# A gated recurrence and a soft mixture of experts on one core: two more couples of units that share their exponential, and another order table

## The chip, the core and the metric

The program runs on one core of a Trainium2 chip, as one launch. The metric is the device time in microseconds (us); lower is better. A core has TensorE (PE in the rows, with PEld for its weight loads), VectorE (DVE), ScalarE (ACT), GpSimd (POOL) and SyncE (SP, which here issues every DMA). All data are float32.

## The reference

Two stages follow each other. The first is a gated linear recurrence along the sequence, for 4 sequences of 5056 tokens with 256 channels:

```python
log_a = 8.0 * sigmoid(r_gate) * log(clip(sigmoid(a_param), 1e-6, 1 - 1e-6))
a_t   = exp(log_a)
norm  = sqrt(maximum(1 - a_t * a_t, 1e-6))
h[t]  = a_t[t] * h[t-1] + norm[t] * sigmoid(i_gate[t]) * x[t]
```

The second takes the 20224 rows h as x of a soft mixture of 8 experts with 4 slots each:

```python
logits   = x @ phi                      # 20224 x 32
d        = softmax(logits, axis=0)      # over all tokens
slot_in  = d.T @ x                      # 32 x 256
slot_out = relu(slot_in[e] @ w1[e]) @ w2[e]
out      = softmax(logits, axis=1) @ slot_out
```

The softmax over all tokens means that no row of the output can be made before the last token has been scanned.

## The kernel before

The 20224 tokens are cut into 40 windows of 512 (the last has 256). Channels are two halves h of 128 partitions. Per window w the program lists operations, each on a given engine, and the texts below name them by these short names:

- `Lr`, `Li`, `Lx` (line 382): three loads of 512 KB on SP.
- `rp` (line 397, PE, per half): the r gate is transposed into a bank of PSUM. `sr` (line 409, ACT, per half): its sigmoid, or a tanh of half the argument, into the buffer A.
- `si` (line 420, ACT): sigmoid of the i gate. `u` (line 432, POOL): that times x.
- `ex` (lines 460 and 462, ACT): the exponential of A in place. Line 460 is used where `sr` ran as a sigmoid, with a scale per channel; line 462 where it ran as a tanh, with a scale and a bias per channel.
- `sq` (line 471, POOL): A squared into buffer N. `qr` (line 478, ACT): the square root of one minus that.
- `up` (line 490, PE, per half): u is transposed into a bank. `st` (line 500, DVE, per half): N times that. `sc` (line 513, DVE, per half): the scan, which carries its last column into the next window.
- `yp` (line 533, PE) and `yc` (lines 286 and 288, a copy on ACT or DVE, two per window): h is transposed back and copied out of PSUM.

Windows are joined to units for `si`, `ex` and `qr`: window 0, (1, 2), (3, 4), 5, and then pairs from (6, 7) to (38, 39); a unit is called by its first window. Four windows make a group g of the second stage: `lp` (line 579, PE, logits), `ls` (lines 588 to 592, DVE, their running maximum), `ep` (lines 603 and 606, PE), `ee` (line 612, ACT, exponential), `md` (line 597, ACT), `acc` (line 621, PE) and `as` (lines 630 and 632, DVE, the sum over tokens).

After the last scan come the end of the sum over tokens (lines 668 to 699: `mp`, `mx`, `mc`, `wj`, `we`, `W`, `sp`, `slot`), the experts (`hp` line 761, `ht` line 773, `so` line 788, all on PE), and then for each group the weights of its tokens (`ct` line 841, `c0` line 847, `cm`, `c1`, `c2`, `c3`), their transposition (`hc` line 865, `hx`), the product (`op` line 894) copied out by ACT or DVE (`og`), and the store (`out`).

ACT holds one table set at a time; tanh and exp are in one set, sigmoid and sqrt each in another, and the build puts a table load ahead of an instruction whose set is not the one held. `EXM` lists couples of units whose `ex` is one operation: it waits for the `sr` of both units. If both units used the same form and their buffers lie fewer than 16 pairs apart, that operation is one instruction per half for both units; otherwise each unit has its own two instructions, one unit behind the other (function `e_ex`).

The order of all operations is written out by hand: `ORDER` is a list of the operations' numbers (a "b" takes the second engine that an operation allows). `Plan.order` goes through it once, gives each operation its buffer, bank or pair from a small model of times, and then the operations are emitted in that order, so that each engine's queue is the table's order of that engine. `LAT["DMA"]` is the model's time between the end of a load's issue and its use; it enters the choice of buffers.

Of the kernel before, what the change touches and what calls it, by code (L numbers as in the profile page):

```python
# [10 lines left out]
ALU = mybir.AluOpType  # L11
# [14 lines left out]

ORDER = """
# [27 lines left out]
790 812 963 986 965 750 771 969 985 751 772 643 661 659 662 675 715 696 682 679 904 905 626 680 683 906 716 756
898 755 737 757 701 908 698 681 684 699 702 700 703 723 720 899 900 739 901 902 624b 798 685 686b 663 664b 909
704 644 705b 665 687 646 896 645b 666b 688b 647b 758 778 759 721 724 722 725 740 799 819 800 742 743 741 903 910
760 911 706 912 707 744 915 913 763 916 726 745 777 779 782 761 764 762 796 747 917 919 765 780 783 781 784 746b  # L60
727b 748b 766 768 728 1089 767b 920 918 729b 978 977 966 791 971 813 979 962 987 983 968 959 957 797 801 804 921
818 820 922 923 924 823 805 802 907 769b 914 803 806 974 972 961 824 821 825 822 982 981 958 988 960 967 976 973
964 980 984 970 785 1067 926 927 786b 807 928 787 937 938 808b 929 788 930 939 946 931 826 827b 940 947 809 810b
941 932 933 942 948 949 943 934 944 935 1090 950 1068 925 951 945 936 952 1013 1111 1035 953 1177 954 1091 990
1112 1113 1000 1114 991b 1036 1014 1037 1038 1039 995 992 996 1005 1001 997 1002 993 1069 1015 1070 1115 1016
1006 1092 998 1071 1017 994 1003 999 1007 1008 1004 1009 1178 1093 1179 1010 955 1116 1040 1018 1094 1072 1041
956 1011 1073 1042 1074 1180 1012b 1055 1056 1057 1059b 1058b 1043 1049 1044 1047 1050 1053 1046b 1045b 1061
1095 1052b 1065b 1096b 1062b 1063b 1051 1181 1064 1075 1076b 1077b 1079 1078 1082 1199 1019 1083b 1086b 1084b
1085 1200 1020 1201 1182 1104 1155 1105b 1107 1156 1097 1157 1133 1108b 1202 1106b 1098b 1099b 1028 1029b 1032b
1031b 1117 1101 1100 1134 1135 1030 1118b 1021 1022b 1024b 1136 1158 1119 1221 1183 1120b 1184b 1122b 1123b 1025  # L70
1023 1121 1159 1160 1126 1161 1127b 1162b 1129b 1128b 1222 1223 1130 1137 1185 1186 1203 1170 1189b 1187b 1188b
1138 1192 1171 1174b 1173b 1224 1172b 1193 1204 1196 1139 1163 1140b 1194b 1195b 1148 1164 1167 1165 1225 1149
1150 1205 1226 1151b 1152b 1166 1206b 1214 1215 1218 1217 1216b 1060 1048 1054 1066 1227 1228b 1141 1207 1208b
1209b 1210b 1142 1143 1145 1211 1144 1229 1236 1230 1231 1237 1240 1233 1239 1238b 1232b 1080 1081 1087 1088
1110 1103 1109 1033 1102 1034 1026 1124 1027 1125 1131 1132 1175 1191 1190 1176 1153 1197 1168 1220 1219 1147
1213 1198 1242 1234 1235 1146 1154 1212 1169 1241
"""


# [96 lines left out]
def kernel(  # L176
# [11 lines left out]
    nc = tc.nc  # L188
# [44 lines left out]
    def Bk(key):  # L233
        return banks[plan.place[key]]
# [4 lines left out]
    def halves(key):  # L239
        return G(key).rearrange("p (h t) -> p h t", h=H)  # L240
# [116 lines left out]
    def window(w):  # L357
# [148 lines left out]

        def e_sc(h):
            def emit(o):
                up = Bk(("up", w, h))
                for s0, s1 in zip(cuts[:-1], cuts[1:]):  # L510
                    init = 0.0 if (w * C + s0) % S == 0 else last_col[h]
                    dst = halves(("A", w))[:, h, s0:s1]
                    nc.vector.tensor_tensor_scan(  # L513
                        dst, dst, up[:, s0:s1], init, op0=ALU.mult, op1=ALU.add
                    )
                    last_col[h] = halves(("A", w))[:, h, s1 - 1 : s1]
            return emit

        for h in range(H):
            op(("up", w, h), "PE", 0.5 * f, e_up(h), deps=[("u", w), ("ident",)],  # L520
               alloc=[("B", ("up", w, h))], uses=[("x", w)])
            op(("st", w, h), "DVE", 0.06 + 0.54 * f, e_st(h), deps=[("up", w, h), ("qr", u0)],
               uses=[("N", w), ("up", w, h)])
            op(("sc", w, h), "DVE", 0.09 * (len(cuts) - 1) + 1.09 * f, e_sc(h),
               deps=[("st", w, h), ("sc", w - 1, h)],
               uses=[("A", w), ("up", w, h)] + ([("A", w - 1)] if w else []))

        def e_yp(i):
            def emit(o):
# [436 lines left out]
```

## Time and profile before

| | us |
|---|---|
| median of 3 runs | 302.04 |
| lowest and highest | 301.23, 302.51 |
| profiled execution, its own time | 301.67 |
| span of its instructions | 299.80 |

Busy time in that span: DVE 239.7 us (80%), ACT 242.2 (81%), PE 234.7 (78%), POOL 181.9 (61%). The DMA queue moved 100.03 MB, at 334 GB/s over the span.

The program has three stretches: up to about 218 us the windows are scanned; up to about 243.5 us the sum over tokens ends and the experts run; after that the output is made and stored. A busy share over the whole span mixes these; it says little on which engine sets the time of one of them.

### The profile page before, as it was taken

The page shows a single profiled execution, that of the slowest core. Times are in us where ns is not written, and L with a number is a line of the kernel's source. Part 1 is how long each engine was busy: PE and PEld are TensorE (multiplying, and loading weights), DVE is VectorE, ACT ScalarE, POOL GpSimd, SP SyncE. Part 2 cuts the span into 40 slices and gives each one's busy share as a digit, 9 for nine tenths or more (in the row PEclk, how much of TensorE's full clock was granted, in tenths as well). Part 3 has the DMA queues.
Part 4 walks back from the last instruction along what each step waited for, and adds up shares of the span by engine and source line. Part 5 has one row for each costly group of instructions (what it writes and reads, how often), then busy time and mean ns, then how long its engine had stood idle before and what let it go on. Part 6 is the DMA issues. An engine that isn't in the chain of part 4 may idle for free.

```text
span 299.8 us, 5788 instructions
## 1 busy us (share of the span) xinstructions
PE 234.7 (78%) x2140; PEld 166.0 (55%) x2140; DVE 239.7 (80%) x379; ACT 242.2 (81%) x303; POOL 181.9 (61%) x122
## 2 busy tenths in 40 slices
PE   3605788869896989799958996899999999898200
PEld 3505575666773967457647663557573677665100
DVE  1003999899999999989999999999968779889600
ACT  5899999999999999999999999999323248885100
POOL 4299579988498898899749898798000421121000
PEclk9975999979999899979999999999999999999755
DMA  6999999799895988859998789999991019999997
GB/s 247 416 410 407 410 397 382 306 390 359 327 416 206 416 340 330 302 200 382 331 360 318 273 302 404 385 378 380 339 398 60 3 79 402 404 402 407 404 378 297
DMA packets 28032, 100.03 MB, mean 334 GB/s; under 512 B 3362, under 2 KB 3364, under 8 KB 28004
## 3 DMA queue, kind: packets, MB, share of 16 engines
q1 hardware_dynamic: 28004, 99.66, 86.7%
q8 instruction: 17, 0.28, 0.4%
q14 instruction: 11, 0.09, 0.1%
HBM read 78.94 MB, written 20.71 MB: 332 GB/s over the span
## 4 chain that ended last, share of the span: by engine, by line
ACT 28%; PE 27%; POOL 15%; issue 12%; DVE 7%; DMA 4%; DVEq 0%; POOLq 0%; ACTq 0%
POOL g L471 8%; POOL g L432 5%; ACT g L462 4%; ACT g L420 4%; ACT g L478 4%; PE b L397 4%; ACT y L286 4%; ACT g L409 4%; PE b L894 4%; DMA g<-in_x_dram 4%; PE b L533 3%; PE b L490 3%; DVE g L288 3%; PE b L788 2%; PE b L761 2%
## 5 line engine op out<-in xcount | busy, mean ns | idle before, releaser
L432 POOL TENSOR_TENSOR g<-g 128x1024 f32<-128x1024 f32 (+1 forms) x40 | 92.7, 2344 | 18.9 <-ACT g L420 17.2
L513 DVE TENSOR_TENSOR_SCAN g<-g,b 128x512 f32<-128x512 f32 (+4 forms) x86 | 98.7, 1175 | 0.4
L471 POOL TENSOR_TENSOR g<-g 128x1024 f32<-128x1024 f32 (+1 forms) x40 | 73.8, 1873 | 17.9 <-ACT g L462 13.6
L500 DVE SCALAR_TENSOR_TENSOR b<-g,b 128x512 f32<-128x512 f32 (+1 forms) x80 | 51.8, 675 | 25.1 <-PE b L490 24.1
L490 PE MATMUL b<-ident,g 128*128 128x128 f32 x316 | 48.5, 289 | 22.0 <-POOL g L432 20.2
L490 PEld LDWEIGHTS b<-ident,g 128*128 128x128 f32 x316 | 36.3, 146 | 35.0 <-POOL g L432 23.6
L397 PE MATMUL b<-ident,g 128*128 128x128 f32 x316 | 46.7, 293 | 6.0 <-DMA g<-in_r_gate_dram 3.7
L533 PE MATMUL b<-ident,g 128*128 128x128 f32 x316 | 44.7, 284 | 8.3 <-DVE g L513 6.8
L397 PEld LDWEIGHTS b<-ident,g 128*128 128x128 f32 x316 | 37.9, 151 | 15.7 <-issue 4.2
L533 PEld LDWEIGHTS b<-ident,g 128*128 128x128 f32 x316 | 35.8, 144 | 18.8 <-DVE g L513 11.2
L409 ACT ACTIVATE g<-b 128x512 f32<-128x512 f32 (+1 forms) x80 | 42.4, 604 | 2.9 <-PE b L397 2.9
L861 POOL TENSOR_TENSOR y<-y,rs 128x512 f32<-128x512 f32 x10 | 10.4, 1047 | 53.5 <-DVE g L779 25.2
L462 ACT ACTIVATE g<-g,ca 128x1024 f32<-128x1024 f32 (+2 forms) x30 | 39.1, 1371 | 0.0
L420 ACT ACTIVATE g<-g 128x2048 f32<-128x2048 f32 (+2 forms) x22 | 37.9, 1744 | 0.1
L478 ACT ACTIVATE g<-g 128x2048 f32<-128x2048 f32 (+2 forms) x22 | 36.8, 1732 | 0.1
L288 DVE COPY y<-b 128x512 f32<-128x512 f32 x53 | 34.6, 680 | 2.1 <-PE b L533 1.5
L286 ACT COPY g<-b 128x512 f32<-128x512 f32 (+1 forms) x45 | 22.2, 567 | 8.7 <-PE b L894 8.0
L894 PE MATMUL b<-soR,y 32*128 32x256 f32 x320 | 27.2, 405 | 1.2 <-ACT y L286 0.7
L288 DVE COPY g<-b 128x512 f32<-128x512 f32 (+1 forms) x43 | 24.7, 629 | 2.5 <-ACT y L286 0.8
L286 ACT COPY y<-b 128x512 f32<-128x512 f32 x36 | 20.0, 601 | 5.7 <-PE b L533 4.4
L621 PE MATMUL b<-y,e 128*32 128x257 f32 x316 | 22.9, 388 | 1.2 <-ACT e L612 1.2
L579 PE MATMUL b<-g,phi_sb 128*32 128x512 f32 (+1 forms) x160 | 22.4, 622 | 0.0
(86 smaller groups left out, 220.2 us busy)
## 6 DMA issues: line engine op xcount, KB each, us to landing
g<-in_i_gate_dram SPq DMA_DIRECT2D x39, 512.0 KB, 7.1
g<-in_x_dram SPq DMA_DIRECT2D x39, 512.0 KB, 6.5
out_dram<-g SPq DMA_DIRECT2D x39, 512.0 KB, 6.4
g<-in_r_gate_dram SPq DMA_DIRECT2D x38, 512.0 KB, 6.5
g<-in_moe_w_dram SPq DMA_DIRECT2D x32, 512.0 KB, 6.2
g<-in_r_gate_dram SPq DMA_DIRECT2D x3, 256.0 KB, 5.0
g<-in_i_gate_dram SPq DMA_DIRECT2D x1, 256.0 KB, 4.2
g<-in_x_dram SPq DMA_DIRECT2D x1, 256.0 KB, 7.7
```

The costliest lines, as they stand in the source:

```text
L286: nc.scalar.copy(out=dst, in_=srct)
L288: nc.vector.tensor_copy(out=dst, in_=srct)
L397: nc.tensor.transpose(out=by_tile(rp, n)[:, j, :], in_=rows(("r", w), n)[:, j, h * P : (h + 1) * P], identity=ident,)
L409: nc.scalar.activation(halves(("A", w))[:, h, :c], Bk(("rp", w, h))[:, :c], f, scale=k)
L420: nc.scalar.activation(a, a, AF.Tanh if twice else AF.Sigmoid, scale=0.5 if twice else 1.0)
L432: nc.gpsimd.tensor_tensor(out=rows(("x", w), n), in0=rows(("i", w), n), in1=rows(("x", w), n), op=ALU.mult)
L462: nc.scalar.activation(a, a, AF.Exp, scale=ca[:, h : h + 1], bias=ca[:, h : h + 1])
L471: nc.gpsimd.tensor_tensor(out=halves(("N", w))[:, :, :c], in0=a, in1=a, op=ALU.mult)
L490: nc.tensor.transpose(out=by_tile(up, n)[:, j, :], in_=rows(("x", w), n)[:, j, h * P : (h + 1) * P], identity=ident,)
L500: nc.vector.scalar_tensor_tensor(up, halves(("N", w))[:, h, :c], 5e-4 if twice else 1e-3, up, op0=ALU.max, op1=ALU.mult)
L513: nc.vector.tensor_tensor_scan(dst, dst, up[:, s0:s1], init, op0=ALU.mult, op1=ALU.add)
L533: nc.tensor.transpose(out=yp[:, j, h * P : (h + 1) * P], in_=halves(("A", w))[:, h, (2 * i + j) * P : (2 * i + j + 1) * P], identity=ident,)
```

## The change

`EXM` gets two more couples, (8, 6) and (28, 24); `LAT["DMA"]` goes from 2.0 to 3.0; and `ORDER` is replaced by another table, with 1241 operations in place of 1243 since each new couple makes one `ex` of two. A second form of the step after the square root (`pooled`) is added to `window`, for windows in the list `BY_POOL`; the list is empty, so that none of its operations is made. Lines of the kernel move down by up to 27.

```diff
-EXM = [(12, 14), (18, 20), (30, 34), (36, 38)]
+EXM = [(8, 6), (12, 14), (18, 20), (28, 24), (30, 34), (36, 38)]
 LAST = 3
+BY_POOL = []
...
-LAT = {"DVE": 0.13, "ACT": 0.15, "POOL": 0.12, "PE": 0.26, "DMA": 2.0}
+LAT = {"DVE": 0.13, "ACT": 0.15, "POOL": 0.12, "PE": 0.26, "DMA": 3.0}
...
-5 1 33 55 11 115 74 96 116 34 13 56 12 75 97 138 35 137 57 178 200 76 159 98 219 241 160 179 201 117 0 3 6 7 8 9
+1 5 74 96 33 115 55 11 35 34 56 57 179 12 76 13 178 0 3 6 7 8 9 10 77 79 101 99 78 102 80 100 36 38 118 58 60 37
...
+        pooled = w in BY_POOL
+        least = 5e-4 if twice else 1e-3
...
+            if pooled:
+                continue
```

Three places show how the instructions move.

The first is ACT's queue around the exponentials of units 6, 8 and 10. Before (the table load, `ex` of 8, a sigmoid, `ex` of 6, `ex` of 10, which is the tanh form, and sigmoids):

```order
L420 ACTIVATE g<-g 128x2048
L409 ACTIVATE g<-b_76 128x512
L460 ACT_TABLE_LOAD
L460 ACTIVATE g<-g,ca_91 128x2x512 x2
L409 ACTIVATE g<-b_77 128x512
L460 ACTIVATE g<-g,ca_91 128x2x512 x2
L462 ACTIVATE g<-g,ca 128x2x512 x2
L409 ACTIVATE g<-b_76 128x512
```

With the change (lines 461, 463, 410 and 421 are the 460, 462, 409 and 420 of before; line 639 is `ee`):

```order
L421 ACTIVATE g<-g 128x2048
L461 ACT_TABLE_LOAD
L461 ACTIVATE g<-g,ca_91 128x2x2x512 x2
L410 ACTIVATE g<-b_75 128x512
L410 ACTIVATE g<-b_77 128x512
L410 ACTIVATE g<-b_76 128x512
L639 ACTIVATE e_68<-b_73 128x512
L463 ACTIVATE g<-g,ca 128x2x512 x2
```

Units 8 and 6 are now two instructions of twice the width, and `ee` of group 0 has come ahead of the exponential of unit 10.

The second is ACT's queue around the couple (12, 14). Before, one joint pair of instructions (the third row), then a sigmoid, `md`, `ee`, the second sigmoid of window 20 and `ex` of 16:

```order
L409 ACTIVATE g<-b_75 128x512
L462 ACT_TABLE_LOAD
L462 ACTIVATE g<-g,ca 128x2x2x512 x2
L409 ACTIVATE g<-b_73 128x512
L597 ACTIVATE d_127<-m_104,n_116 128x1
L612 ACTIVATE e_68<-b_77 128x512
L409 ACTIVATE g<-b_72 128x512
L462 ACTIVATE g<-g,ca 128x2x512 x2
```

With the change:

```order
L421 ACTIVATE g<-g 128x2048
L461 ACT_TABLE_LOAD
L461 ACTIVATE g<-g,ca_91 128x2x512 x2
L463 ACTIVATE g<-g,ca 128x2x512 x2
L410 ACTIVATE g<-b_73 128x512
L639 ACTIVATE e_68<-b_75 128x512
L410 ACTIVATE g<-b_71 128x512
L410 ACTIVATE g<-b_72 128x512
L624 ACTIVATE d_127<-m_104,n_116 128x1
```

The couple's two units have different forms now and are four instructions; the sigmoid right behind them is the first of window 26 (into bank b_73), which stood behind `ex` of 16 before.

The third is the end of the scans. On DVE before, around `as` of group 7 (line 632), which stands between the `st` of window 38 and its `sc`:

```order
L513 SCALAR_TENSOR_TENSOR g<-g,b_71 128x512
L500 SCALAR_TENSOR_TENSOR b_70<-g,b_70 128x512
L500 SCALAR_TENSOR_TENSOR b_74<-g,b_74 128x512
L632 SCALAR_TENSOR_TENSOR accS<-accS,d_133,b_77 128x257
L513 SCALAR_TENSOR_TENSOR g<-g,b_74 128x512
```

With the change it stands ahead of the first `st` of window 36 (the fourth row):

```order
L504 SCALAR_TENSOR_TENSOR b_75<-g,b_75 128x512
L659 SCALAR_TENSOR_TENSOR accS<-accS,d_133,b_74 128x257
L528 SCALAR_TENSOR_TENSOR g<-g,b_75 128x512
L504 SCALAR_TENSOR_TENSOR b_70<-g,b_70 128x512
L528 SCALAR_TENSOR_TENSOR g<-g,b_70 128x512
```

On PE, between the last `acc` and the experts, before (841 is `ct`, 696 is `sp`, 761 is `hp`):

```order
L841 MATMUL b_75<-ident,l_78 128x4x32 x4
L841 MATMUL b_77<-ident,l_82 128x4x32 x4
L841 MATMUL b_73<-ident,l_79 128x4x32 x4
L696 MATMUL b_74<-Wt,accS 128x32 x2
L841 MATMUL b_71<-ident,l_85 128x4x32 x4
L761 MATMUL b_74<-g,slotT 32x512 x8
```

With the change (868, 723 and 788 are the same three):

```order
L868 MATMUL b_70<-ident,l_80 128x4x32 x4
L868 MATMUL b_74<-ident,l_85 128x4x32 x4
L723 MATMUL b_71<-Wt,accS 128x32 x2
L868 MATMUL b_72<-ident,l_78 128x4x32 x4
L868 MATMUL b_71<-ident,l_81 128x4x32 x4
L788 MATMUL b_76<-g,slotT 32x512 x8
```

One `ct` has moved from ahead of `sp` to behind it.

## Rows read from the trace of the kernel before

**Rows 1.** Busy time by stretch: us, PE, PEld, DVE, ACT, POOL, PEclk, DMA share, GB/s.

```profile
27.60:201.60 174.00, 150.24 (x1281) 108.58 (x1280) 169.11 (x231) 172.89 (x185) 146.88 (x72) 0.97 0.91 345
201.60:218.40 16.80, 16.29 (x144) 10.98 (x143) 16.55 (x30) 10.88 (x19) 7.10 (x4) 1.00 0.96 354
243.50:299.80 56.30, 33.83 (x368) 23.56 (x368) 35.47 (x68) 27.18 (x56) 5.23 (x5) 0.83 0.94 369
```

**Rows 2.** Waits of ACT between 4 and 217 us: total us, times, longest us.

```profile
ACT y L286 <- PE b L533: 4.4, 2, 2.4
ACT g L409 <- PE b L397: 2.9, 4, 1.2
```

**Rows 3.** Timeline of ACT, pieces of six stretches: start us, us, what, count.

```profile
46.17 2.19 ACT L460 ACTIVATE g<-g,ca 128x1024 f32<-128x1024 f32 x2
48.27 0.57 ACT L409 ACTIVATE g<-b 128x512 f32<-128x512 f32 x1
...
132.85 2.37 ACT L462 ACTIVATE g<-g,ca 128x1024 f32<-128x1024 f32 x2
135.11 1.07 ACT L409 ACTIVATE g<-b 128x512 f32<-128x512 f32 x2
...
164.80 4.08 ACT L462 ACTIVATE g<-g,ca 128x2048 f32<-128x2048 f32 x2
168.77 2.60 ACT L409 ACTIVATE g<-b 128x512 f32<-128x512 f32 x6
...
196.05 0.35 ACT L597 ACTIVATE d<-m,n 128x1 f32<-128x1 f32 x1
196.25 2.09 ACT L286 COPY y<-b 128x512 f32<-128x512 f32 x4
198.35 1.28 ACT L478 ACT_TABLE_LOAD   x1
199.65 3.38 ACT L478 ACTIVATE g<-g 128x2048 f32<-128x2048 f32 x3
```

**Rows 4.** Timeline of DVE at the end of the scans.

```profile
201.59 1.29 DVE L500 SCALAR_TENSOR_TENSOR b<-g,b 128x512 f32<-128x512 f32 x2
...
210.79 0.48 DVE L632 SCALAR_TENSOR_TENSOR accS<-accS,d,b 128x257 f32<-128x257 f32 x1
...
218.25 0.14 DVE L661 COPY m<-m 32x1 f32<-32x1 f32 x1
```

**Rows 5.** Waits of DVE between 28 and 218 us.

```profile
DVE b L500 <- ACT g L478: 0.7, 1, 0.7
```

**Rows 6.** Timeline of ACT, its first sigmoids; in brackets the idle time before.

```profile
5.97 0.60 ACT L409 ACTIVATE g<-b 128x512 f32<-128x512 f32 x1 [1.16 <-PE b L397]
6.83 0.60 ACT L409 ACTIVATE g<-b 128x512 f32<-128x512 f32 x1 [0.26 <-PE b L397]
8.37 2.07 ACT L409 ACTIVATE g<-b 128x512 f32<-128x512 f32 x4 [0.94 <-PE b L397]
```

**Rows 7.** The chain of work that ended last, at the experts' start: start us, us, what.

```profile
222.09 1.86 PE b L841 x12
223.95 0.37 PE b L696 x4
224.32 0.54 PE b L841 x4
224.86 5.29 PE b L761 x48
```

**Rows 8.** Timeline of ACT around the couple (12, 14).

```profile
71.85 1.95 ACT L420 ACTIVATE g<-g 128x2048 f32<-128x2048 f32 x1
73.66 1.12 ACT L409 ACTIVATE g<-b 128x512 f32<-128x512 f32 x2
...
76.09 4.08 ACT L462 ACTIVATE g<-g,ca 128x2048 f32<-128x2048 f32 x2
```

**Rows 9.** The loads of line 382, from issue to landing.

```profile
DMA to landing us min/median/max: 3.3/6.6/11.7
```

More of the change, by code (lines that the diff above doesn't have):

```diff
@@ new lines @@
+598 653 613 633 618 615 616 617 619 891 890 602 604 639 892 655 636 562 603 620 581 583 634 654 635 716 736 582b
+605b 717 564 565b 584b 675 695 563 893 895 658 958 978 980 749 708 667 689 730 960 707 977 729 673 676 640 637
+641 638 642 752 644 656 659 657 660 680 681 682 902 903 694 696 699 677 748 769 789 970 770 969 966 971 965 957
+788 810 713 754 896 753 643b 894 796 904 714 735 755 906 645 678 700 697 679 698 718 897 898 701 721 899 900 901
+740 661 683 621 685 662b 684b 686b 622b 623 624b 907 702 737 663 704 905 703b 719 722 720 738 723 739 664b 908
@@ new lines @@
+909 758 910 911 761 741 913 1033 912 742 756 776 757 762 797 817 775 798 794 743 914 763 759 915 724 726 780
+744b 727b 725b 781 760 782 917 918 777 745 764 766 778 779 746b 765b 705b 767b 963 979 976 811 982 959 964 981
+967 973 987 956 961 962 955 795 802 799 919 816 803 920 821 921 922 818 1109 783 800 801 804 819 822 820 823 968
+986 975 972 984 983 985 924 925 785 935 805 936 926 806 807 928 784b 786b 927 808b 929 937 916 944 1034 939 945
+824 940 825b 946 923 930 931 932 933 947 941 942 1065 1175 1110 948 949 938 934 943 950 951 952 1011 1087 988
@@ new lines @@
+1066 1067 1111 1012 1013 989 1014 1015 1112 1003 993 990 994 998 995 1004b 1035 991 1036 999b 996 1037 1088 1089
+1090 1068 992 1000 1005 1001 997 1002 1006 1007 1113 1069 1176 1177 1091 953 954 1070 1038 1016 1092 1039 1008b
+1178 1009 1010b 1071 1072b 1040 1041 1042 1043 1047 1044b 1045b 1048 1049 1051b 1050b 1053 1059 1054b 1061b
+1063b 1093 1094b 1056 1055 1057 1060 1062 1179 1073 1074 1077 1075b 1076b 1080 1153 1017 1131 1081b 1084b 1018b
+1082b 1083b 1154 1155 1132 1133 1102 1156 1026 1103b 1105b 1106b 1104 1157 1027 1030 1029b 1028b 1095 1096b
@@ new lines @@
+1098b 1134 1099b 1097b 1180 1181 1182 1135 1197 1019 1020b 1022b 1021 1158 1136 1114 1159 1160b 1183 1137 1219
+1198 1199 1184b 1185b 1023b 1187 1190 1138 1200 1186 1220 1115 1191b 1192b 1116b 1193b 1221 1194 1146 1168 1147b
+1150b 1148b 1201 1149 1161 1169b 1172b 1171 1170 1162b 1165 1164b 1202 1163b 1203 1117 1118 1121 1204b 1120b
+1119b 1124 1125 1126 1127b 1128b 1046 1052 1058 1064 1139 1205 1222 1140b 1142b 1143b 1141 1212 1206b 1223 1208
+1213b 1215b 1207b 1224 1209 1214 1225 1216 1226 1227 1234 1235 1237 1228b 1231b 1236b 1229b 1238 1230 1078 1079
@@ L77 @@
+1085 1086 1107 1108 1031 1032 1100 1101 1024 1189 1188 1195 1196 1152 1174 1166 1173 1025 1123 1167 1129 1130
+1145 1211 1218 1122 1239 1232 1233 1144 1217 1240 1210 1151
 """
@@ L500, in emit, with e_uc, e_nm, e_pb @@
                 nc.vector.scalar_tensor_tensor(
-                    up, halves(("N", w))[:, h, :c], 5e-4 if twice else 1e-3, up, op0=ALU.max, op1=ALU.mult
+                    up, halves(("N", w))[:, h, :c], least, up, op0=ALU.max, op1=ALU.mult
                 )
             return emit
+        def e_uc(h):
+            return lambda o: copy(o, halves(("x", w))[:, h, :c], Bk(("up", w, h))[:, :c])
+        def e_nm(o):
+            nt = halves(("N", w))[:, :, :c]
+            nc.gpsimd.tensor_scalar(nt, nt, least, None, op0=ALU.max)
+        def e_pb(o):
+            b = halves(("x", w))[:, :, :c]
+            nc.gpsimd.tensor_tensor(out=b, in0=halves(("N", w))[:, :, :c], in1=b, op=ALU.mult)
         cuts = [0] + [b * S - w * C for b in range(1, B) if w * C < b * S < w * C + c] + [c]
@@ L508, in emit @@
             def emit(o):
-                up = Bk(("up", w, h))
+                b = halves(("x", w))[:, h, :] if pooled else Bk(("up", w, h))
                 for s0, s1 in zip(cuts[:-1], cuts[1:]):
@@ L513, in emit @@
                     nc.vector.tensor_tensor_scan(
[L514 removed]
+                        dst, dst, b[:, s0:s1], init, op0=ALU.mult, op1=ALU.add
                     )
@@ L526, in window @@
                uses=[("A", w), ("up", w, h)] + ([("A", w - 1)] if w else []))
+        if pooled:
+            op(("nm", w), "POOL", 0.08 + 0.95 * f, e_nm, deps=[("qr", u0)], uses=[("N", w)])
+            for h in range(H):
+                op(("uc", w, h), ("ACT", "DVE"), {"DVE": 0.06 + 0.54 * f, "ACT": 0.055 + 0.43 * f}, e_uc(h),
+                   deps=[("up", w, 0), ("up", w, 1)], uses=[("x", w), ("up", w, h)])
+            op(("pb", w), "POOL", 0.08 + 1.77 * f, e_pb, deps=[("nm", w), ("uc", w, 0), ("uc", w, 1)],
+               uses=[("N", w), ("x", w)])
+            for h in range(H):
+                op(("sc", w, h), "DVE", 0.09 * (len(cuts) - 1) + 1.09 * f, e_sc(h),
+                   deps=[("pb", w), ("sc", w - 1, h)], uses=[("A", w), ("x", w)] + ([("A", w - 1)] if w else []))
         def e_yp(i):
```

39 lines of the change are left out of this document (7 added, 32 removed), and 31 rows, old and new, of the table ORDER.

## The prediction

> **What bounds the kernel now.** I first read the busy time by stretch, then each engine's waits, then the timelines of the two engines that turned out full. The busy shares of the whole span (ACT 81%, DVE 80%) hide that between 27.6 and 201.6 us ACT is busy for 172.89 of 174.00 us and DVE for 169.11 [rows 1]. POOL and PE have room there, and the DMA share is 0.91. The waits of ACT say the same: 2.9 us in four waits for a transposed gate, and 4.4 us for y copies, which come at 213 us and later, when its main work is over [rows 2]. Of the 2.9 us, 1.16, 0.26 and 0.94 stand before its first sigmoids [rows 6], so that one wait of about 0.5 us is left for the other 190 us. DVE waited only 0.7 us for a square root [rows 5].
>
> The two engines meet at the root of unit 36. The last three roots start at 199.65 us [rows 3], the first of them takes about 1.9 us, and DVE's first `st` of window 36 starts at 201.59 us [rows 4], when DVE has just run out of earlier work. From there DVE has its last eight `st`, eight scans and the end of the maximum, to 218.25 us [rows 4], with 16.55 of 16.80 us busy [rows 1]. Then the experts follow on PE from 224.86 us [rows 7], and then the output, whose 56.3 us are DMA time (share 0.94, 369 GB/s) while ACT is busy for 27 and DVE for 35 us [rows 1]. So the time is: ACT's queue up to the root of 36, DVE's tail, the experts, the stores.
>
> **ACT's work up to that root.** Counting the order's rows to that point, both versions have 80 `sr`, 20 `si`, 20 `qr`, 8 `ee` and 22 table loads (24 in the whole program). The new couples spare no table load. What differs: one y copy more (20 for 19), four of which take 2.10 us up to the next instruction, so 0.5 [rows 3]; one `md` more, 0.20 (196.05 to 196.25) [rows 3]; and the exponentials. A joint couple in the tanh form takes 3.97 us (164.80 to 168.77), a single unit in that form 2.26 (132.85 to 135.11), a single unit in the sigmoid form 2.10 (46.17 to 48.27) [rows 3]. From unit 6 on, before has 3 joint tanh couples, 3 single sigmoid and 8 single tanh units. The change has six couples, but (28, 24) has its buffers 16 pairs apart and (12, 14) and (18, 20) mix the forms, so that three of the six are single units one behind the other. It comes to 2 joint tanh couples, 1 joint sigmoid couple, 3 single sigmoid and 8 single tanh units. The difference is a joint sigmoid couple for a joint tanh one. No row has that instruction. It can't take more than two single units, 4.20; carried over from the tanh form, less the 0.16 us between the single units, it takes 3.81. I take 3.81, the nearer row, so -0.16, and keep +0.23 as the other end. Sum for ACT: 0.5 + 0.2 - 0.16 = **+0.5 us** (to +0.9).
>
> **The start.** Ahead of the first table load for the sigmoid of i, ACT has the same twelve sigmoids and four units' exponentials in both, in another order. Its waits after the first sigmoid are 0.26 + 0.94 = 1.20 us [rows 6]. Now the second sigmoid is of window 4, third on PE. The second and the fourth transposition set the starts at 6.83 and 8.37, 0.77 us each, so the third gives 7.6. Three sigmoids follow at 0.48 (four in 2.07 us [rows 6]) without a wait, and the fourth ends at about 9.05 in place of 9.33. That is -0.3 if the loads land as they did. I take **-0.2** (0 if they don't, -1.2 if every wait goes).
>
> **The remaining wait.** The one later wait of ACT may go (-0.5) or stay. I take **0**; new waits are a rival. POOL's squares are ahead of the roots in the new order too, and have become freer in two rounds, since a couple of single units releases the first squares before its end.
>
> **DVE's tail.** One `as`, 0.48 us [rows 4], moves from the tail to ahead of window 36. There it is covered: up to that point DVE has two y copies less and this one operation more, and it arrives early and waits for the root anyway. If ACT were early instead, it would count in full. **-0.4** (0 to -0.48).
>
> **The way to the experts.** A `ct` takes 0.62 us (three in 1.86), and `sp` starts when the third is through [rows 7]. With two ahead it could start 0.62 us sooner, if the weights W are there, and then two `ct` in place of one stand between it and the experts. That is 0 if W is early, +0.62 if it is late. All `acc` of group 9 also stand ahead of `mc` now, where two stood behind it. I take **+0.1** (-0.2 to +0.6).
>
> **The loads and the stores.** The same bytes move in another order; the last weights are issued in time for the second expert product, since only three loads instead of six are behind the last one that needs a buffer of the scans. Eight of the output's copies go from DVE to ACT, both with 20 us or more to spare under the DMA's 56.3 [rows 1]. **0** (-0.5 to +0.5).
>
> **Sum:** 0.5 - 0.2 - 0.4 + 0.1 = 0.0 against the profiled execution's own 301.67 us (a span of 299.80 and 1.87 around it). The median of the three runs is 302.04, 0.37 above that execution. I give **301.8**, between the two. What a measurement of this kernel can tell from no change is about 0.5%, 1.5 us.
>
> **Rival one, faster: ACT's last waits go.** If the new load order lets every sigmoid after the first find its gate, 1.2 us at the start and 0.5 us later go, and with the tail's 0.48 and ACT's +0.5 that is -1.7: 300.0 us. For it: four fifths of ACT's waits of 2.9 us [rows 2] stand in the first 9 us [rows 6], and the order of the first loads is another one. Against it: after the first 9 us ACT hardly waits for a load now, so there is half a microsecond to win, and the start is paced by loads that land one behind the other.
>
> **Rival two, slower: the sigmoid of window 26 waits for its load.** Before, it stood behind `ex` of 16; now it is right behind the couple (12, 14). That couple's exponentials began 4.2 us after the sigmoid of i of unit 14, at 76.09 after 71.85 [rows 8]. As four instructions they take 2.10 + 2.26 and end at about 80.4. The load of that r gate goes into the buffer that the second `up` of window 9 frees, which stands on PE behind the transposition of window 23, whose sigmoid ACT takes just ahead of 71.85. So it is issued at about 72, and its transposition (0.7) must be done by 80.4. It decides whether the load lands more than 7.7 us after its issue. Loads landed after 3.3 to 11.7 us, half of them within 6.6 [rows 9]. At 6.6 nothing happens; at 11.7 ACT waits 4.0 us, and PE, where this transposition stands ahead of those of windows 20 and 21, has nothing to give it. I price it at 2.4 us: 304.1. The Trainium skill (DMA: Bandwidth & Descriptors, section Anatomy of one DMA — SWDGE (gpsimd) path), measured on GpSimd's path, puts a transfer at about 2.0 us and its bytes at 436 GB/s, 3.2 us here as an estimate; by that rule this rival is none, and a planner needs no more than the 2.0 it had. The trace agrees with it at its least, 3.3, and not at its median, 6.6 [rows 9]: loads queue behind one another. So the rival stays.
>
> **Chances.** No change within 0.5%: 0.56, the sum and small waits around it. Faster by more: 0.20, the first rival and sums near it. Slower by more: 0.24, of which 0.18 is the second rival and the rest another wait of that kind. The range goes from 300.2, most of the first rival, to 303.9, most of the second; about one in ten is left out on each side.
>
> **What would show it.** In the new profile ACT should be busy for all but 1 to 2 us from its first roots to the root of 36, which should end at 201.5 to 202.0, with DVE now idle for about 1 us more before such roots than the 0.7 of [rows 5]. The joint exponentials of 8 and 6 should take 3.8 us. The end of the maximum should come at 217.9 to 218.4, and the experts at 224.5 to 225.2. The prediction is wrong if ACT shows a wait of over a microsecond for a transposed gate, at window 26 or anywhere else, or if the first `st` of window 36 no longer follows the root directly.

## The result and the profile after

| | before | after |
|---|---|---|
| median, us | 301.96 | 303.25 |
| lowest and highest of 8 runs each | 301.23, 302.51 | 302.69, 303.74 |
| span of the profiled execution | 299.80 | 301.5 |

The ratio is 1.0043, with a 95% interval of 1.0028 to 1.0057. So the change is 1.3 us slower: less than the 0.5% named as telling it from no change, but outside the noise of these runs. The forecast was 301.8, the range 300.2 to 303.9.

Both profiled executions can be laid side by side at five events; all but the first row are distances.

| us | before | after | difference |
|---|---|---|---|
| first `st` of 36 begins | 201.59 | 202.15 | +0.56 |
| to the end of the maximum | 16.80 | 17.45 | +0.65 |
| to the first `hp` | 6.40 | 6.63 | +0.23 |
| to the landing of the last store | 73.88 | 74.08 | +0.20 |

They add up to 1.64 of the 1.7 us between the spans. What was forecast were +0.3, -0.4, +0.1 and 0. The two in the middle are the miss.

Busy time by stretch after (columns as in [rows 1]); the second row is from the first `st` of 36 to the end of the maximum:

```profile
27.60:202.10 174.50, 148.85 (x1287) 108.80 (x1286) 167.92 (x229) 173.38 (x187) 147.52 (x72) 0.98 0.92 345
202.10:219.60 17.50, 16.89 (x141) 10.42 (x141) 16.58 (x29) 11.66 (x19) 7.01 (x4) 1.00 1.02 400
```

ACT is full up to the root, 173.38 of 174.50 us. In the second row PE (the first number, 16.89 of 17.50) is busier than DVE (16.58), though DVE has one `as` less there than before.

ACT after, pieces of its timeline that answer to [rows 3, 6]:

```profile
6.12 0.60 ACT L410 ACTIVATE g<-b 128x512 f32<-128x512 f32 x1 [1.36 <-PE b L398]
7.82 2.06 ACT L410 ACTIVATE g<-b 128x512 f32<-128x512 f32 x4 [1.11 <-PE b L398]
...
45.64 3.90 ACT L461 ACTIVATE g<-g,ca 128x2048 f32<-128x2048 f32 x2
...
68.78 1.57 ACT L410 ACTIVATE g<-b 128x512 f32<-128x512 f32 x3 [0.60 <-PE b L398]
...
133.71 4.64 ACT L463 ACTIVATE g<-g,ca 128x1024 f32<-128x1024 f32 x4
...
200.06 3.38 ACT L479 ACTIVATE g<-g 128x2048 f32<-128x2048 f32 x3
```

The joint exponential of 8 and 6 takes 3.90 us; (28, 24), at 133.71, is four instructions in 4.64 us. ACT waits three times for a gate, twice in the first 8 us and once at 68.78.

DVE after, around the end of the scans, answering to [rows 4] (216.21 is `ls` of group 9), and its waits, answering to [rows 5]:

```profile
200.56 0.48 DVE L659 SCALAR_TENSOR_TENSOR accS<-accS,d,b 128x257 f32<-128x257 f32 x1
200.96 1.27 DVE L528 TENSOR_TENSOR_SCAN g<-g,b 128x512 f32<-128x512 f32 x1
202.15 0.68 DVE L504 SCALAR_TENSOR_TENSOR b<-g,b 128x512 f32<-128x512 f32 x1
...
216.21 0.72 DVE L616 TENSOR_SCALAR_CACHE_REDUCE l<-b,m 96x512 f32<-96x512 f32 x1
...
217.67 0.69 DVE L289 COPY y<-b 128x512 f32<-128x512 f32 x1 [0.48 <-PE b L560]
...
219.47 0.14 DVE L688 COPY m<-m 32x1 f32<-32x1 f32 x1
```

```profile
DVE b L504 <- ACT g L479: 1.6, 4, 0.6
DVE b L504 <- PE b L491: 1.3, 2, 1.0
```

The moved `as` (200.56) wasn't in a gap: the scan behind it ends at 202.23, after the root of 36 (201.97). And at 217.67 DVE, for the first time since 202.15, stands still for PE: 0.48 us, for a `yp` of window 38. Before, it nowhere did so up to the end of the maximum. The waits for roots came to 1.6 us in place of 0.7, as the prediction had said ("about 1 us more"). The chain of waits of that stretch, after:

```profile
213.15 0.48 PE b L868 x4
213.63 0.44 PE b L560 x4
214.06 1.85 PE b L606 x12
215.91 0.59 PE b L560 x4
216.50 0.55 PE b L606 x2
217.05 0.59 PE b L560 x4
217.63 0.55 PE b L606 x2
218.18 0.60 PE b L560 x4
...
220.65 1.87 PE b L648 x24
222.53 0.17 PE b L705 x8
222.69 0.98 PE b L648 x4
223.68 1.17 PE b L868 x8
224.84 0.39 PE b L723 x4
225.23 1.07 PE b L868 x8
```

From 209.7 us on nearly every piece is PE's: `acc` of group 8, `yp` (L560) and `lp` (L606) in turn, `acc` of groups 9 (24 matmuls) and 10 (4), `ct`, `sp`, `ct`. The chain of the kernel before could have told the same: there every piece from 209.81 to 219.61 us is PE's too.

### The profile page after: what moved, and what is told of

It reads as the page before. It is cut to its first block, busy times and chain, and to the rows that moved or that the text cites. A ratio compares the mean times of both kernels' runs of the same rounds, so it can differ in the third digit from the quotient of the medians.

```text
span 301.5 us, 5788 instructions
## 1 busy us (share of the span) xinstructions
PE 232.2 (77%) x2140; PEld 166.0 (55%) x2140; DVE 235.0 (78%) x370; ACT 246.0 (82%) x312; POOL 181.7 (60%) x122
## 4 chain that ended last, share of the span: by engine, by line
ACT 29%; PE 25%; DVE 24%; issue 10%; POOL 3%; DMA 1%; DVEq 0%; SPq 0%; ACTq 0%; POOLq 0%
DVE g L528 10%; ACT g L463 6%; ACT g L410 6%; DVE b L504 5%; PE b L921 4%; ACT g L479 4%; DVE g L289 4%; ACT g L421 3%; PE b L398 3%; DVE y L289 3%; PE b L491 2%; PE b L560 2%; PE b L815 2%; PE b L788 2%; PE b L606 2%
## 5 line engine op out<-in xcount | busy, mean ns | idle before, releaser
L491 PE MATMUL b<-ident,g 128*128 128x128 f32 x316 | 48.9, 289 | 21.9 <-POOL g L433 15.7
L398 PE MATMUL b<-ident,g 128*128 128x128 f32 x316 | 47.1, 290 | 8.4 <-DVE g L528 3.0
L560 PE MATMUL b<-ident,g 128*128 128x128 f32 x316 | 46.0, 283 | 9.3 <-DVE g L528 6.0
L560 PEld LDWEIGHTS b<-ident,g 128*128 128x128 f32 x316 | 35.2, 143 | 21.8 <-DVE g L528 9.5
L463 ACT ACTIVATE g<-g,ca 128x1024 f32<-128x1024 f32 (+2 forms) x28 | 34.8, 1325 | 0.0
L287 ACT COPY g<-b 128x512 f32<-128x512 f32 (+1 forms) x53 | 25.9, 584 | 4.2 <-PE b L921 4.0
L921 PE MATMUL b<-soR,y 32*128 32x256 f32 x320 | 25.6, 401 | 1.3 <-DVE y L289 1.1
L289 DVE COPY g<-b 128x512 f32<-128x512 f32 (+1 forms) x35 | 19.6, 607 | 4.5 <-PE b L921 4.3
L648 PE MATMUL b<-y,e 128*32 128x257 f32 x316 | 22.2, 386 | 0.8 <-ACT e L639 0.8
L921 PEld LDWEIGHTS b<-soR,y 32*128 32x128 f32 x320 | 18.7, 184 | 6.1 <-ACT g L287 1.7
```

The lines of the kernel that those rows point to most:

```text
L398: nc.tensor.transpose(out=by_tile(rp, n)[:, j, :], in_=rows(("r", w), n)[:, j, h * P : (h + 1) * P], identity=ident,)
L463: nc.scalar.activation(a, a, AF.Exp, scale=ca[:, h : h + 1], bias=ca[:, h : h + 1])
L491: nc.tensor.transpose(out=by_tile(up, n)[:, j, :], in_=rows(("x", w), n)[:, j, h * P : (h + 1) * P], identity=ident,)
L560: nc.tensor.transpose(out=yp[:, j, h * P : (h + 1) * P], in_=halves(("A", w))[:, h, (2 * i + j) * P : (2 * i + j + 1) * P], identity=ident,)
L921: nc.tensor.matmul(Bk(("op",) + tag + (n,))[:, i * D : (i + 1) * D], hT()[r, (2 * i2 + i) * P : (2 * i2 + i + 1) * P], soR[r, :], start=Tr ...
```

## The experiments

Theory A was that the order behind the first `st` of 36 loses the time, B that the new couples do, C that loads and stores do. D and E came later and are told where they are first used. In the edits `acc 9.2` is the `acc` of group 9, column block 2, `yc 38.0` the first copy of window 38, `st 36.1` the `st` of its second half, and the lines show the order on the engines named. Each run stands beside runs of the kernel before on the same chip. The last column of this table names those profiled executions in which the granted clock between 58 and 91 us was 1.00 and not 0.95; why that shifts the first `st` by some 0.7 us is told in the last section. Distances behind it can be compared all the same. A ratio is known to some 0.0015, half a microsecond; what is read from smaller differences rests on one trace each.

| | ratio to before, 95% interval | first `st` of 36 | to end of maximum | to `hp` | to last store | clock |
|---|---|---|---|---|---|---|
| after | 1.0043 [1.0028, 1.0057] | 202.15 | 17.45 | 6.63 | 74.08 | |
| x1 | 0.9985 [0.9968, 1.0002] | 201.53 | 16.69 | 6.40 | 73.84 | 1.00 |
| x2 | 1.0139 [1.0114, 1.0164] | 203.47 | 18.78 | 6.69 | 74.37 | 1.00 |
| x3 | 1.0048 [1.0029, 1.0067] | 202.21 | 17.74 | 6.68 | 74.17 | |
| x4 | 1.0016 [0.9995, 1.0036] | 201.34 | 17.13 | 6.59 | 74.30 | 1.00 |
| x5 | 1.0020 [1.0005, 1.0035] | 201.31 | 17.24 | 6.90 | 73.89 | 1.00 |
| x6 | 1.0039 [1.0023, 1.0055] | 201.60 | 16.70 | 7.42 | 74.01 | 1.00 |
| x7 | 1.0001 [0.9983, 1.0019] | 202.59 | 16.70 | 6.04 | 74.10 | |
| x8 | 1.0040 [1.0024, 1.0056] | 201.87 | 17.46 | 6.63 | 74.19 | 1.00 |
| x9 | 1.0040 [1.0027, 1.0054] | 202.26 | 17.45 | 6.39 | 74.35 | |
| x10 | 1.0012 [0.9997, 1.0028] | 202.01 | 17.45 | 6.26 | 74.21 | |
| x11 | 1.0013 [1.0001, 1.0025] | 201.77 | 16.80 | 6.94 | 73.85 | |
| x12 | 0.9992 [0.9972, 1.0012] | 201.37 | 17.76 | 6.34 | 73.91 | |
| x13 | 1.0019 [1.0008, 1.0030] | 201.29 | 16.29 | 7.08 | 74.19 | 1.00 |
| x14 | 1.0001 [0.9989, 1.0012] | 202.21 | 16.70 | 6.20 | 73.86 | |
| x15 | 1.0009 [0.9992, 1.0026] | 200.84 | 17.72 | 6.12 | 73.93 | 1.00 |
| x16 | 1.0010 [0.9999, 1.0020] | 201.37 | 17.45 | 6.63 | 74.36 | |
| x17 | 0.9968 [0.9950, 0.9986] | 201.53 | 16.69 | 6.40 | 73.80 | |
| x18 | 0.9959 [0.9942, 0.9977] | 201.00 | 16.78 | 6.17 | 74.11 | |

**x1 and x2: the two tables crossed.** Cut at the first `st` of 36; operations that only one of the two tables has behind the cut count as behind it.

```diff
-behind the first st of 36: the change's order
+behind the first st of 36: the order of before
```

> The changed kernel up to the first st of window 36, from there on the order of before. Theory A (the end of the scans and the way to the experts lose the time): the root of 36 still ends at about 202.0 us, but the end of the maximum comes back from 219.47 to about 218.7 and the experts from 226.23 to 225.3, and the time falls from 303.25 by 0.8 to about 302.4. Theory B (the new couples and the order ahead of the root lose it): nothing moves after the root, the time stays at 303.2. Theory C (the loads of weights and the stores lose it): the experts come earlier, but the last store doesn't, the time stays at 303.2.

> The kernel before up to the first st of window 36, from there on the order of the change. Theory A: the root of 36 ends at 201.6 us as before, the experts come 0.8 to 1.0 us later than before, at about 225.8, and the time is 301.96 + 0.8 = 302.8. Theory B: 302.0. Theory C: about 302.0 to 303, with the experts where they were and the last store later.

x1 falls to 0.9985: undoing everything behind that point takes back the whole loss. It has 23.09 us from the first `st` to `hp`, before has 23.20 and the change 24.08. B falls for the largest part. From C the ratio can't tell, since x1 has the old order of the last loads and of the stores too; the distances put 1.0 us ahead of `hp` and 0.24 us behind it. x2 is a miss: 306.42 us, 3.4 above the highest number given. Its ACT shows why:

```profile
201.45 1.28 ACT L597 ACT_TABLE_LOAD   x1
202.74 0.29 ACT L597 ACTIVATE d<-m,n 128x1 f32<-128x1 f32 x1
203.05 1.28 ACT L478 ACT_TABLE_LOAD   x1
```

The `as` that the change puts ahead of 36 needs `md` of group 7, which in the crossed table fell between the roots of 36 and 38: two more table loads, and DVE waiting 2.37 us for that `md`. This kernel tells nothing of A.

**x3: hand-overs on DVE.**

```diff
 DVE: st 36.1
-sc 36.1, st 36.0, ls 8, st 37.1, sc 36.0, sc 37.1, st 37.0, sc 37.0, st 38.1, st 38.0, sc 38.0, sc 38.1
+st 36.0, sc 36.1, ls 8, st 37.1, sc 36.0, st 37.0, sc 37.1, sc 37.0, st 38.1, st 38.0, sc 38.1, sc 38.0
 PE: up 37.1
-ep 8, up 37.0
+up 37.0, ep 8
```

> The changed kernel, with no scan right behind its own st in the end (windows 36 to 38: both st, then both sc). Theory A: three hand-overs from an operation to one that needs it cost 0.10, 0.12 and 0.19 us on DVE, where independent ones overlap by about 0.1 us; ls of group 9 begins about 0.4 us sooner after the first st of 36. The copy of window 38 behind it still waits for PE, so only a part comes through: 302.9 to 303.25. Theories B and C: 303.25.

Nothing is won. DVE now waits for PE:

```profile
205.72 0.70 DVE L504 SCALAR_TENSOR_TENSOR b<-g,b 128x512 f32<-128x512 f32 x1 [0.16 <-PE b L491]
...
218.01 0.69 DVE L289 COPY y<-b 128x512 f32<-128x512 f32 x1 [0.75 <-PE b L560]
```

`ls` of group 9 begins 14.05 us after the first `st`, in the change 14.06: what the hand-overs gave back was slack in front of PE, whose order this edit changes as well. That DVE's own order costs nothing is not shown. In x5 below DVE has no wait for PE up to the end of the maximum, and that end still comes 17.24 us after the first `st`, before 16.80; DVE is idle there for 0.46 us ahead of a scan of window 38.

**x4: the last logits on PE.**

```diff
 PE: lp 10.0
-yp 38.0, lp 10.1
+lp 10.1, yp 38.0
 DVE: ls 9
-yc 38.0, ls 10
+ls 10, yc 38.0
```

> The changed kernel, with the second logits of group 10 ahead of the y transposition of window 38 on PE, and the last step of the maximum ahead of the copy of window 38 on DVE. Theory A: the maximum ends at about 218.7 instead of 219.47, and as the copy of window 38 comes 0.5 us later for the last sums, 0.4 to 0.8 us of it reach the experts: 302.4 to 302.9. Theories B and C: 303.25.

The maximum ends 0.32 us sooner after the first `st`, not 0.77: the copy of window 38 now stood between `ls` and the last step of the maximum. The ratio falls by 0.0027, 0.8 us, of which the distances show 0.14; the intervals overlap a little.

**x5, x6 and x7: one section at a time.**

```diff
 x5: the change
-from the end of the maximum on, its own order
+from the end of the maximum on, the order of before
 x6: x1
-from the end of the maximum on, the order of before
+from the end of the maximum on, the change's order
 x7: x1
-from the first hp on, the order of before
+from the first hp on, the change's order
```

> The changed kernel up to the end of the maximum, from there on (the way to the experts, the experts, the output) the order of before. Theory A, by the traces: from the end of the maximum to the experts 6.63 us in the change against 6.40 before, and from the experts to the last store 74.08 against 73.88, so 0.4 us come back: 302.8 by the median of the change, and the end of the maximum stays where the change has it, 17.4 us after the first st of 36 (before 16.8). If the whole loss sits in the way, 301.7 to 302.

> The changed kernel up to the first st of 36, then the order of before up to the end of the maximum, and from there that of the change. Theory A: the end of the maximum comes 16.8 us after the first st, and 0.7 to 1.3 us come back: 302.0 to 302.6. If the whole loss sits in the way to the experts: 303.2.

> The kernel of x1 (new order up to the first st of 36, then that of before, 301.75 us), with the order of the change from the first expert product on. Theory A: the stores differ by 0.2 us, so 301.75 to 302.0. Theory C (the output's order loses the time): 302.5 or more.

x5 gets its number by luck: the way to `hp` did not come back to 6.40 but grew to 6.90. x6 misses: its maximum ends in 16.70 us, as expected, and then the way to `hp` takes 7.42. In both the cut took two `ct` out of PE's queue ahead of the end of the maximum and put them between `ep` and the last sums, 1.0 us in the chain of waits of either kernel; 16.70 + 7.42 and 17.24 + 6.90 come to the change's 24.1. So these two runs can't divide the loss between the sections. They do show how the sections hang together: with two `ct` fewer on PE the maximum ends no sooner in x6 (16.70, in x1 16.69) and 0.21 us sooner in x5, and the `ct` are paid for behind it. That led to theory D: the loss is the order of the queue that runs through both sections, PE's above all. In x7 the output's order costs 0.26 us from `hp` to the last store; its ratio stands 0.0016 above x1, with intervals that overlap. (Its way to `hp` is shorter, as two `c0` of DVE went behind `hp` with the cut.)

**x8: the couples.**

```diff
-EXM = [(8, 6), (12, 14), (18, 20), (28, 24), (30, 34), (36, 38)]
+EXM = [(12, 14), (18, 20), (30, 34), (36, 38)]
 ACT:
-ex 8+6 ... ex 28+24
+ex 8, ex 6 ... ex 28, ex 24
```

> The changed kernel without the two new couples: units 8 and 6, and 28 and 24, have each its own two exponentials again, one unit behind the other in the same place. Theory A: only the joint sigmoid couple spared anything, 3.9 against 4.2 us; ACT's root of 36 ends 0 to 0.3 us later, 303.25 to 303.55. Theory B (the couples lose the time, since a unit waits for its partner): 302.5 to 302.8.

1.0040 against 1.0043: by the ratio the couples neither cost nor bring anything. B falls. The traces without a fall of the clock show a little: the root of 36 ends at 201.69 us here and at 201.17 and 201.13 in x4 and x5, which have the couples; some 0.3 us of it is the joint pair of (8, 6), the rest stands ahead of it. On (28, 24) as a joint pair this run says nothing, since it wasn't one in the change (see x16).

**x9, x10 and x11: the `acc` of the last two groups.** PE after, then PE of x1 (which has the order of before there):

```profile
220.58 1.94 PE L648 MATMUL b<-y,e 128*32 128x257 f32 x24
222.46 0.24 PE L705 MATMUL b<-ones,mmax 1*32 1x1 f32 x8
222.62 1.05 PE L648 MATMUL b<-y,e 128*32 128x257 f32 x4
```

```profile
219.36 1.07 PE L648 MATMUL b<-y,e 128*32 128x257 f32 x12
220.36 0.24 PE L705 MATMUL b<-ones,mmax 1*32 1x1 f32 x8
220.53 1.08 PE L648 MATMUL b<-y,e 128*32 128x257 f32 x16
```

12 matmuls of three windows take 1.07 us and 16 of four windows 1.08; but the four of the fourth window alone take 1.05. Each window writes its own 32 output rows, and in these rows those of different windows run side by side. The Trainium skill (TensorEngine Tiling (Array Packing), section Key Properties) says that different tiles can execute weight loads and matmuls in parallel; the trace agrees, 16 in the time of 12. The change put `acc 10` by itself.

```diff
 x9, PE: acc 9.0, acc 9.1
-acc 9.2, acc 9.3, mc, acc 10.0, acc 10.1
+acc 10.0, acc 9.2, acc 10.1, acc 9.3, mc
 x10, PE: acc 9.0, acc 9.1
-acc 9.2, acc 9.3, mc, acc 10.0, acc 10.1
+mc, acc 10.0, acc 9.2, acc 10.1, acc 9.3
 x11, the kernel before, PE: acc 9.0, acc 9.1
-mc, acc 10.0, acc 9.2, acc 10.1, acc 9.3
+acc 9.2, acc 9.3, mc, acc 10.0, acc 10.1
```

> The changed kernel with the two acc of group 10 (window 39, the fourth block of 32 columns) put between those of group 9 (three windows, the first three blocks), as before had it; mc stays behind them all. Theory D (from the exponential of group 8 to the experts PE's queue is the bound, and acc of group 10 costs 1.05 us by itself where beside group 9 it costs nothing): sp ends 0.6 us sooner than 225.23, the time is 302.6. Theory E (the chain maximum, weights, W on DVE is the bound there): the experts stay at 226.2, 303.2.

> As x9, and mc (the maximum handed to all rows) ahead of the second half of group 9's acc, the whole order of before for these seven operations. Theory D: the weights come in time as well, the experts begin 0.9 us sooner, at 225.3, the time is 302.3 to 302.5. Theory E: the same, as mc is now 0.9 us earlier; x9 alone tells D from E.

> The kernel before, with the seven operations in the order of the change: all four acc of group 9, then mc, then the two acc of group 10. Theory D: acc of group 10 takes 1.05 us by itself and the experts begin 0.7 to 0.9 us later than 224.79; the time is 1.002 to 1.003 of before. Theory E: mc is 0.9 us later, the experts 0.3 to 0.9 us later.

By the traces x9 wins 0.24 us on the way to `hp` where 0.6 was expected, x10 0.37 where 0.9 was, and x11 loses 0.54. x9's ratio, 1.0040, doesn't show its part. In x9 PE is done sooner and `sp` waits for the weights W, which wait for `mc`: so E holds a part, and the acc and `mc` have to move together. x10's ratio is 0.0031 below the change's, more than its trace explains. The kernel before, with these seven operations in the change's order, is slower by 0.0001 to 0.0025.

**x12, x14 and x15: what bounds the end of x1.**

```diff
 x12, PE:
-yp 29.1, yp 33.0, up 35.0
+up 35.0, yp 29.1, yp 33.0
 x12, ACT (yc 33.1 was DVE's):
-yc 33.0, yc 31.1, qr 36, qr 38, si 38
+yc 31.1, qr 36, qr 38, yc 33.0, yc 33.1, si 38
 x14, DVE:
-wj, c0 2, as 8, as 10, as 9
+as 8, wj, c0 2, as 10, as 9
 x14, PE:
-ct 0, ct 4, ct 1, sp, ct 7
+ct 0, ct 4, sp, ct 1, ct 7
 x15: x14, with the PE edit of x12; ACT:
-yc 36.0, ee 8
+ee 8, yc 36.0
```

> The kernel of x1, with the second operand of window 35 transposed one place sooner on PE (ahead of the y transposition of window 29, where DVE waited 0.76 us for it), and the two copies of window 33 on ACT behind the root of 38 instead of ahead of the root of 36 (ACT) and of the first st of 36 (DVE). Theory D: DVE reaches the first st of 36 at 200.5 to 201.0 us instead of 201.53, and the root of 36 ends at 200.3; PE, full from about 201 us on, gives back part of it: 0.3 to 0.9 us less than x1, 300.9 to 301.5. If PE alone bounds the end: 301.75.

> The kernel of x1 with as of group 8 ahead of wj on DVE, in a gap of 1.2 us, and sp ahead of ct of group 1 on PE. Theory D: W ends 0.4 us sooner and sp 0.6 to 0.9, and the experts begin 0.4 us sooner, at 6.0 us after the end of the maximum in place of 6.4: 0.9970 to 0.9985 of before. If another chain bounds there: as x1, 0.9985.

> As x14, with the second operand of window 35 transposed one place sooner (as in x12), and the exponential of group 8 on ACT ahead of a y copy. No copy stands behind the root this time. Theory D: the first st of 36 comes 0.5 us sooner than in x1, and since PE's sums of group 8 no longer wait for ACT, 0.2 to 0.5 us of it reach the experts: 0.9955 to 0.9975 of before. If PE is full all through, as x14.

All three miss. x14 has its 0.2 us on the way to `hp` in the trace, half of what was expected, and no ratio to show it. x12 and x15 do start the `st` of 36 sooner, by 0.7 us in x15, and give all of it back before the end of the maximum (17.7 us for 16.7). x15's trace says where, on PE and then on DVE:

```profile
208.67 1.06 PE L491 MATMUL b<-ident,g 128*128 128x128 f32 x8 [0.86 <-ACT e L639]
```

```profile
209.84 1.29 DVE L504 SCALAR_TENSOR_TENSOR b<-g,b 128x512 f32<-128x512 f32 x2 [0.89 <-PE b L491]
```

The transposition of window 38 had been given the bank that the exponential of group 8 frees. An edit of the order also deals out the eight banks anew.

**x13: four places of the change mended.**

```diff
 PE: x4's and x10's edits
 DVE: ls 9
-yc 38.0, ls 10, mall, c0 1, mx
+ls 10, mall, yc 38.0, mx
 DVE: wj
+c0 1
```

(`mall` is the copy that ends the maximum.)

> The changed kernel with four places of its end mended: the acc and mc as before (x10), the two logits of group 10 together on PE, the last step of the maximum ahead of the copy of window 38 on DVE, and c0 of group 1 behind wj. Theory D (the loss is the order of PE's and DVE's queues from the last scans to the experts): hp starts 23.2 us after the first st of 36, as before, in place of 24.1, and the time is 302.2 to 302.5, 1.000 to 1.001 of before. If the loss sits elsewhere (the stores, ACT's root): 1.003 or more.

The way from the first `st` to `hp` falls from 24.08 to 23.37, 0.7 of the 0.9 us between the change and before. The ratio, 1.0019, lies between the two answers that I had written down. The stores keep the change's order there, 0.3 us longer than before.

**x16, x17 and x18: the load time, and a version that beats both.**

```diff
 x16 (the change), x17 (x1), x18 (x14 with x12's PE edit)
-LAT = {"DVE": 0.13, "ACT": 0.15, "POOL": 0.12, "PE": 0.26, "DMA": 3.0}
+LAT = {"DVE": 0.13, "ACT": 0.15, "POOL": 0.12, "PE": 0.26, "DMA": 2.0}
 x18, PE:
-ct 3, up 38.0, up 38.1
+up 38.0, up 38.1, ct 3
```

> The changed kernel with the load time of the model back at 2.0: the same order, other buffers, by which the couple (12, 14) or another mixed one becomes one pair of instructions and the couple (8, 6) keeps its own. All theories: 0 to 0.3 us less by the joint pair, 302.9 to 303.25; a new wait of a load on its buffer, if the model's 3.0 was needed, would show as ACT idle before a sigmoid: 303.5 or more.

> The kernel of x1 (new order up to the first st of 36, then that of before) with the load time of the model at 2.0, by which the couple (28, 24) comes to lie 3 pairs apart and becomes one pair of instructions. x16 had unit 24's root 0.6 us sooner after that of 12 than the change (57.07 against 57.65 us). Theory D: ACT's root of 36 and all behind it come 0.5 us sooner than in x1: 0.9965 to 0.9975 of before, 301.2 us. If PE bounds the end whatever comes sooner: as x1, 0.9985.

> As x17, with the sums as in x14, the second operand of window 35 sooner as in x15, and ct of group 3 behind the operands of window 38 on PE, so that neither of them gets the bank that the exponential of group 8 frees (in x15 PE waited 0.86 us for that one, and DVE 0.89 behind it). Theory D: DVE's wait before st of 38 goes and the experts begin 0.3 to 0.8 us sooner than in x17: 0.9945 to 0.9970 of before. If the sums of group 8 on PE, behind the exponential of group 8, bound it: as x17.

With 2.0 the buffers of (28, 24) lie 3 pairs apart, not 16, and the couple becomes one pair of instructions in x16:

```profile
133.51 4.08 ACT L463 ACTIVATE g<-g,ca 128x2048 f32<-128x2048 f32 x2
```

That is 0.56 us under the 4.64 of the change, and the root of 24 follows that of 12 after 57.07 us in place of 57.65. (The expectation named the wrong couple and gave 0 to 0.3.) No new wait for a load shows: ACT waited 2.9 us for gates in x16, 3.1 in the change. The ratio falls further than that, by 0.0033 or 1.0 us, and the two intervals lie apart. x17 adds it to x1: 0.9968, with intervals that overlap. In x18 the wait of x15 ahead of window 38 is gone, and from the first `st` of 36 to the first `hp` it takes 22.95 us, with the first `st` 0.5 us sooner than in x17. It ran at 301.09 us, 0.9959 [0.9942, 0.9977] of before, faster than both kernels; against x17 alone the intervals overlap.

## Why the prediction was wrong

- **What bounds the kernel.** Right up to the root of 36: ACT is full, and the root came 0.41 us later (201.97 for 201.56, both in profiles with a fall of the clock) where +0.3 was forecast. Wrong behind it. The sentence that failed is that the time is "ACT's queue up to the root of 36, DVE's tail, the experts, the stores". The row of [rows 1] that I read for DVE, 16.55 of 16.80 us, says 16.29 for PE. Two engines were full there, and I costed the moves on one of them. The kernel before, on PE and then on DVE (`lp` and `ls` of group 9):

```profile
213.48 1.92 PE L579 MATMUL b<-g,phi_sb 128*32 128x512 f32 x12
```

```profile
215.49 0.75 DVE L589 TENSOR_SCALAR_CACHE_REDUCE l<-b,m 96x512 f32<-96x512 f32 x1
```

PE ended at 215.40, 0.09 us ahead of the `ls` that needs it. So a DVE freed of 0.48 us of work had hardly 0.1 us to gain as long as PE's queue stayed as it was.

- **DVE's tail, -0.4: the step that failed.** Measured +0.65, and the bounds of 0 to -0.48 didn't hold it. Freeing DVE of an `as` freed nothing: `ls` of group 9 begins 14.06 us after the first `st` (216.21), before 13.90, as hand-overs from `st` to `sc` took up what the `as` had left and PE was close behind (x3). The other 0.48 of the 0.65 is the wait for a `yp` at 217.67. What the new order did with PE's queue wasn't costed at all: a `yp` between the two `lp` of group 10, a third `yp` ahead of `ep` of group 9, and on DVE a copy that waits for one of them ahead of the last `ls` (x4 and x13 put the two `lp` side by side again and the copy behind the last `ls`). The `as` was also not covered where it went: DVE was busy until 202.23, later than the root, so that the first `st` came 0.56 us later and not 0.41.
- **The way to the experts, +0.1.** Measured +0.23, inside its bounds, but I had priced a `ct` and noted the `acc` without a price. x11 gives that one, 0.54 us; other moves there gave some of it back.
- **ACT's work.** Up to the next instruction, as the forecast counts, the joint sigmoid couple took 3.81 us (45.64 to 49.45), just the forecast. I gave `LAT` no price of its own, though I had seen that (28, 24) were 16 pairs apart; x16 prices that at 0.56 us by its trace. It is a gain that the change gave away and no miss of the sum, which counted that couple as four instructions.
- **The start, -0.2.** The first sigmoid of i ended 0.05 us sooner: the second wait is 1.11 us, as the second gate now is the third on PE, and the four sigmoids behind it then run without one.
- **The stores, 0 (±0.5).** +0.20 in the trace, 0.26 in x7.
- **The rivals.** Neither came. ACT has no wait at window 26, where rival two put it, but that was close: its load landed 7.4 us after its issue, and the rival needed more than 7.7. The time came out slower by PE's queue, which no rival named. Of the two signs of being wrong, the wait of over a microsecond stood at the start (1.36 and 1.11 us) and told nothing, as before had one of 1.16 there; the other, the `st` held back behind the root, came with 0.18 us.

The loss can be undone in two ways: by the old order behind the first `st` of 36 (x1, a ratio 0.0058 lower) or by the old load time (x16, 0.0033 lower); both together give 0.0075 (x17). By that ratio the new order up to there, with the old load time, wins something (of which the spans, 299.6 us in x17 and 299.8 before, show little), and the order behind it and `LAT` took more than that. How the time divides among the places behind the first `st` isn't settled to a tenth: sections of one queue don't add (x5, x6), and x13, which mends four of them, takes back 0.7 us by its trace, while its interval overlaps the change's.

## What to carry to other kernels

Read every engine's busy time in the stretch that you cost: where two are full, taking work off one buys next to nothing (DVE's `as` in the change, two `ct` of PE in x6), and a move has to be priced on both, with the buffers that it deals out anew. Small matmuls into separate blocks of 32 output rows belong next to each other in the queue; one block left alone costs as much as four together (1.05 and 1.08 us). A parameter that only feeds a model of the order (here the load time) can undo what the change is named after, so look for its effect in the instructions.

## What was not expected of the hardware

The same instructions in the same order got one of two clocks. The change, and then x4, which has the same order up to 200 us, in four slices of 2 us (columns as in [rows 1]; the number before the last two is the granted clock):

```profile
62.00:64.00 2.00, 0.62 (x4) 0.38 (x4) 2.00 (x3) 1.98 (x2) 2.00 (x2) 1.00 1.01 391
64.00:66.00 2.00, 1.13 (x9) 0.92 (x10) 2.00 (x4) 1.99 (x2) 1.42 (x1) 1.00 0.96 328
66.00:68.00 2.00, 2.00 (x12) 1.70 (x11) 1.55 (x3) 2.00 (x5) 1.69 (x1) 0.54 0.92 354
68.00:70.00 2.00, 2.00 (x13) 2.00 (x12) 1.87 (x2) 1.40 (x4) 2.00 (x2) 0.60 0.95 379
```

```profile
62.00:64.00 2.00, 0.54 (x4) 0.30 (x4) 2.00 (x3) 1.98 (x2) 2.00 (x2) 1.00 1.03 404
64.00:66.00 2.00, 1.21 (x9) 1.00 (x10) 2.00 (x4) 1.99 (x2) 1.35 (x1) 1.00 0.98 328
66.00:68.00 2.00, 1.83 (x16) 1.42 (x15) 2.00 (x3) 2.00 (x6) 1.78 (x1) 1.00 1.02 404
68.00:70.00 2.00, 2.00 (x21) 2.00 (x20) 2.00 (x4) 2.00 (x5) 2.00 (x2) 1.00 1.01 367
```

PE does little between 62 and 66 us in both. In the change the clock then falls to mostly the lower of its two levels (1.2 and 2.4 GHz), a gate is late, and ACT, the full engine, waits 0.60 us at 68.78; in x4 the clock stays and ACT has no such wait. What decides between the two isn't shown. From the root of 6 to that of 12 it takes 31.2 to 31.5 us in the twelve profiled executions with the fall, before and after among them, and 30.6 to 30.7 in the eight without. So the wait of "about 0.5 us" that the prediction left with ACT is of this kind (0.55 us at 67.17, before), and some 0.7 us of a span here are chance: two profiles must be compared piece by piece.
